# A multi-head attention block on one Trainium2 core: one output tile taken out of the planned order, and a small mask product moved from VectorE to GpSimd

## The chip, the core and the metric

The kernel runs on one core of a Trainium2 chip. A core has five engines that run side by side, each with its own instruction queue worked off in order: TensorE (PE in the profile; its weight loads are PEld), VectorE (DVE), ScalarE (ACT), GpSimd (POOL) and SyncE (SP), which here only issues DMAs. They meet through semaphores. The metric is the device time of one execution in microseconds (us); a program's time is the median over its runs.

## The reference

```python
B, S, D, H = 1, 2048, 448, 16          # x (B, S, D), wqkv (D, 3D), wo (D, D), all bf16
qkv = (x @ wqkv) -> (3, B, H, S, Dh)   # Dh = 28
scores = einsum("bhqd,bhkd->bhqk", q, k) * Dh ** -0.5
p = softmax(scores)
o = einsum("bhqk,bhkd->bhqd", p, v)
return o.reshape(B, S, D) @ wo
```

## The kernel before, in words

**Tiles.** The 16 heads form 4 groups `g` of 4 heads; the 2048 queries form 4 blocks `c` of 512 (`QW`); the keys form 16 tiles of 128. One group and one query block make a window `w = 4g + c`, 16 in all, worked off in that order. A score tile is 128 keys by 512 queries of one head (`emit_S`, L854), and there are 4 x 4 x 16 x 4 = 1024 of them. Softmax takes no maximum over scores: a bound for each key is put into spare rows of the key operand `KB` and the query operand `QB`. The key half of that bound is a mask times the largest absolute key value, `NK` (L615, 128 x 128), copied into `KB` by four DMAs (L613) for each of the groups 1 to 3.

**Exponentials.** Most score tiles come in pairs in one of two double banks `PA[0]`, `PA[1]`; ScalarE takes e^x of both at once into a tile of `PTA` (L1277, 422 times). The remaining 181 go to one of the single banks `PD[0..2]`. There VectorE and GpSimd compute the exponential together: either VectorE twice (L1058, L1061), a product on GpSimd (L1064, tile `DG`), VectorE once (L1077, tile `PTD`), 157 times; or one copy on VectorE (L990) and six GpSimd instructions (L997 to L1020), 24 times.

**Value products.** Four heads of one key tile are multiplied with the values into the accumulator bank `PO` (L1122, four matmuls side by side). At a window's end VectorE copies `PO` to `OSB` (L942), the softmax sums travel by DMA (L949, L952, L954, ending in `RRB`), and GpSimd writes the normalized result `OT[g][c]` (L957).

**Output.** For a query block `c`, four output tiles `tq` of 128 queries are each a sum over the four groups of `OT[g][c]` times `WO[:, g, :]`. `SPLIT` lists the tiles whose groups 0 to 2 are summed ahead (`task_part`, L788, kept by VectorE at L791 in unused halves of key tiles); for those `task_OP` later multiplies group 3 alone (L804) and VectorE adds the kept part (L808). For a tile that isn't in `SPLIT`, all four groups are summed in `task_OP` and VectorE copies the result (L811). One DMA on SP then writes the block's four tiles (L817).

**The end.** The last window, group 3 of block 3, has no later window to hide behind. Its groups 0 to 2 are summed into the three `PD` banks by `late_sums` (L888, output tiles 0, 1 and 3 = `ACCQ`); output tile 2 has its part in `PARTL`. Behind the last value product, code outside the planned order follows: VectorE transposes `PO` (L866), takes reciprocals (L867), and for each half of the queries transposes them back (L870) and multiplies (L1399); TensorE multiplies with `WO` (L1401), ScalarE copies tiles 0, 1, 3 (L1407), VectorE adds tile 2 (L1405), and four DMAs write them (L1408; the last from ScalarE's queue).

**Order.** Nothing is scheduled by hand or by the framework. A planner inside the kernel simulates the five engines with fixed costs for each operation (`Op`, `try_pe`, `try_act`, `try_static`, and the loop that calls them): whenever an engine is free it takes a ready operation, by `prio` and some rules of its own, so that a small change of one duration can change much of what follows. The list `log` of what was taken then becomes each engine's instruction order. At run time only that order is kept, and instructions start when their semaphores allow.

Of the kernel before, what the change touches and what calls it, by code (L numbers as in the profile page):

```python
# [10 lines left out]
ALU = mybir.AluOpType  # L11
# [7 lines left out]
P = 128  # L19
H = 16  # L20
HP = 32
G = 4
HG = 4
CC = 4
QW = 512
# [57 lines left out]
def kernel(  # L83
# [7 lines left out]
    nc = tc.nc  # L91
    _, S, D = x.shape
    Dh = D // H
    CK = D // CC
    NQC = S // QW
    NKT = S // P
    TPC = QW // P
# [53 lines left out]
    LOOK = 0.2  # L151
    SLK = 0.13
    MG = 0.1
    SPLIT = {2: (0, 1, 2, 3), 3: (2,)}
    ACCQ = (0, 1, 3)
    ACCP = 2000
    PARTD = 60
# [37 lines left out]
    out_perm = out[0][QW:S].rearrange("(p t) d -> p t d", t=NKT - TPC)  # L195
# [15 lines left out]
    WO = sb([P, G, D], BF16, "WO")  # L211
# [7 lines left out]
    KMAX = [sb([P, 1], F32, f"KMAX{g}") for g in range(G)]  # L219
    NK = [sb([P, P], BF16, f"NK{g}") for g in range(G)]  # L220
    VA = [sb([P, NKT, HG, HP], BF16, f"VA{g}") for g in range(G)]
    OT = [[sb([P, QW], BF16, f"OT{g}_{c}") for c in range(NQC)] for g in range(G)]
# [19 lines left out]
    OUTS = XS  # L242

    PA = [psum.tile([P, UA * QW], F32, name=f"PA{i}") for i in range(NA)]
    PD = [psum.tile([P, QW], F32, name=f"PD{i}") for i in range(ND)]
# [11 lines left out]
    maskm = sb([P, QW], BF16, "maskm")  # L257
# [61 lines left out]
    log = []  # L319
# [9 lines left out]
    def add(op):  # L329
        static[op.eng].append(op)  # L330
        return op

    def bank_task():
        return {"slot": None}
# [232 lines left out]
    def task_kmax(g):  # L567
        due = g * 4 * WT - 40
        prio = -4100 if g == 0 else due - 1000
        elig = None  # L570
        m = add(Op("DVE", 0.12, lambda: nc.vector.tensor_reduce(out=KMAX[g][:], in_=KPART[g][:], axis=AX.X, op=ALU.max),
                   deps=kmaxop[g], prio=prio, elig=elig))

        kmax_op.append(m)
        if g == 0:
            nk = add(Op("DVE", 0.2, lambda: nc.vector.tensor_scalar(
                out=NK[0][:], in0=maskm[:, 0:P], scalar1=KMAX[0][:, 0:1], scalar2=RK0[:, 0:1], op0=ALU.mult, op1=ALU.mult),
                deps=[m] + rk_op, prio=prio + 0.2))
            for n, (c0, c1) in enumerate(KCH):
                for i in range(HG):  # L580
                    o = add(Op("SP", DISS, (lambda i=i, c0=c0, c1=c1: nc.sync.dma_start(
                        out=KB[0][i // 2][HP * SI[i]:HP * (SI[i] + 1), c0 * QW:c1 * QW],
                        in_=KB[1][0][HP * SI[i]:HP * (SI[i] + 1), c0 * QW:c1 * QW])),
                        deps=[k0ev[sc] for sc in range(c0, c1)], prio=-2000 + 20 * n + i, lat=DLAT + 0.3))
                    k0mv.append(o)
                    for sc in range(c0, c1):
                        kev[(g, sc, i)] = o

            def rep0(i, c0, c1):
                st = SI[i] ^ 1  # L590
                nc.sync.dma_start(out=KB[0][i // 2][HP * st:HP * (st + 1), c0 * QW:c1 * QW].rearrange("p (r q) -> p r q", q=P),
                                  in_=NK[0][HP * SI[i]:HP * (SI[i] + 1), None, :].to_broadcast([HP, (c1 - c0) * QW // P, P]))
            for n, (c0, c1) in enumerate(RCH):
                for i in range(HG):
                    o = add(Op("SP", DISS + 0.07, (lambda i=i, c0=c0, c1=c1: rep0(i, c0, c1)), deps=[nk],
                               prio=(-1990 + 20 * n if c0 else -300) + 0.1 * i, lat=DLAT + 0.6, elig=None if c0 else lambda t: pos[0] >= NF * FB * HG + 4))
                    for c in range(c0, c1):
                        kmrep[(g, c, i)] = o
            return
        deps = []  # L600
        c0 = 0
        for st in (1, 3):
            o = add(Op("SP", DISS, (lambda st=st: nc.sync.dma_start(
                out=KB[g % 2][1][HP * st:HP * (st + 1), c0 * QW:S], in_=KB[g % 2][0][HP * st:HP * (st + 1), c0 * QW:S])),
                deps=[kev[(g, sc, 0)] for sc in range(c0, NQC)], prio=due + 0.01 * st, lat=DLAT + 0.3))
            deps.append(o)
            for sc in range(c0, NQC):
                kev[(g, sc, 2 + st // 2)] = o

        def rep_out(i, c0):  # L610
            st = SI[i] ^ 1
            n = (S - c0 * QW) // P
            nc.sync.dma_start(out=KB[g % 2][i // 2][HP * st:HP * (st + 1), c0 * QW:S].rearrange("p (r q) -> p r q", q=P),  # L613
                              in_=NK[g][HP * SI[i]:HP * (SI[i] + 1), None, :].to_broadcast([HP, n, P]))
        nk = add(Op("DVE", 0.2, lambda: nc.vector.tensor_scalar(  # L615
            out=NK[g][:], in0=maskm[:, 0:P], scalar1=KMAX[g][:, 0:1], scalar2=None, op0=ALU.mult), deps=[m], prio=prio + 0.2, elig=elig))
        for i in (2, 3, 0, 1):
            o = add(Op("SP", DISS + 0.07, (lambda i=i: rep_out(i, c0)), deps=[nk] + ([deps[i]] if i < 2 else []),
                       prio=due + 0.3 + 0.001 * i, lat=DLAT + 0.6))
            for c in range(c0, NQC):  # L620
                kmrep[(g, c, i)] = o
# [174 lines left out]
    def task_OP(c):  # L796
        due = (12 + c + 1) * WT + 16
        st = add(Op("SP", 0.05, None, prio=due))
        evs = []
        for tq in range(TPC):  # L800
            task = bank_task()
            ap = (lambda task=task: bank(task)[:, 0:D])
            g0 = G - 1 if c in SPLIT else 0
            ops = chain_mm(G - g0, lambda k, tq=tq, ap=ap: nc.tensor.matmul(  # L804
                out=ap(), lhsT=OT[g0 + k][c][:, tq * P:(tq + 1) * P], rhs=WO[:, g0 + k, :], start=(k == 0), stop=(g0 + k == G - 1)),
                [ot_done[(g, c)] for g in range(g0, G)], due + tq * 10, None, acq_d(task, urgent=NT - UO))
            if g0:
                ev = add(Op("DVE", 0.56, lambda tq=tq, ap=ap: nc.vector.tensor_tensor(  # L808
                    out=OUTS[c][:, tq, :], in0=ap(), in1=part(c, tq), op=ALU.add), deps=[ops[-1], parts[(c, tq)]], prio=due - 1000))
            else:  # L810
                ev = add(Op("DVE", 0.54, lambda tq=tq, ap=ap: nc.vector.tensor_copy(out=OUTS[c][:, tq, :], in_=ap()),  # L811
                            deps=[ops[-1]], prio=due - 1000))
            def aft(t, task=task):
                task["slot"].free_at = t + SEM
            ev.after = aft
            evs.append(ev)
        add(Op("SP", 0.05, lambda: nc.sync.dma_start(out=out_perm[:, c * TPC:(c + 1) * TPC, :], in_=OUTS[c][:]),  # L817
               deps=evs, prio=due))

    SEGS = [(FB * w, FB * (w + 1)) for w in range(NF)] + [(FB * NF + (NKT - FB) * w, FB * NF + (NKT - FB) * (w + 1)) for w in range(NF)]  # L820

# [18 lines left out]
    acts = []  # L840
# [22 lines left out]
    late_acc = {}  # L863

    def norm_dve(src, dt, dr, den, then):
        nc.vector.transpose(out=dt, in_=src)  # L866
        nc.vector.reciprocal(out=dr, in_=dt[:, Dh::HP])  # L867
        n = QW // HP // 2
        for hf in range(2):
            nc.vector.transpose(out=den(hf), in_=dr[:, hf * n:(hf + 1) * n].rearrange("p (n o) -> p n o", o=1).to_broadcast([P, n, HP]))  # L870
            then(hf)
# [508 lines left out]
    log.sort(key=lambda e: (e[0], e[1]))  # L1380
    sync = mybir.DependencyInfo(mybir.DependencyClass.Sync, mybir.DependencyReason.DATA)
    issued = []
    for _, _, o in log:
        if o.fn is None:
            continue
        r = o.fn()
        if o.eng == "DVE" and r is not None:
            issued.append((o, r))
        elif o.eng == "POOL" and o.kind in ("p", "n", "g"):
            before = [d for d in issued[-8:] if d[0].end <= o.start + 1e-6 and (d[0].kind == "sb" or d[0].end <= o.start - PLD + 1e-6)]  # L1390
            if before:
                tc.add_manual_dep(r.ins, before[-1][1].ins.name, sync)
    c = NQC - 1
    g = G - 1
    hw = QW // 2
    fb = {tq: PD[late_acc[tq]][:, 0:D] if tq in late_acc else PA[1 - acts[-1][2].idx][:, 0:D] for tq in range(TPC)}

    def half_out(hf):
        nc.vector.tensor_tensor(out=OTL[hf], in0=PO[:, hf * hw:(hf + 1) * hw], in1=DEN[hf], op=ALU.mult)  # L1399
        for tq in (2 * hf, 2 * hf + 1):  # L1400
            nc.tensor.matmul(out=fb[tq], lhsT=OTL[hf][:, (tq % 2) * P:(tq % 2 + 1) * P], rhs=WO[:, g, :], start=(tq not in late_acc), stop=True)  # L1401
    norm_dve(PO[:], DT[:], DR[:], lambda hf: DEN[hf], half_out)
    for tq in range(TPC):
        if tq in SPLIT[c]:
# [31 lines left out]
```

## Time and profile before

| | |
|---|---|
| time, median of 3 runs (lowest to highest) | 410.15 us (410.08 to 410.36) |
| span of the profiled execution | 408.4 us |
| ScalarE busy | 394.3 us, 97% |
| VectorE busy | 382.0 us, 94% |
| TensorE matmul busy | 359.9 us, 88% |
| GpSimd busy | 329.2 us, 81% |

The span runs from the first to the last instruction of one profiled execution; the time of a run is measured from outside and is some 1.75 us longer. An engine row gives busy time, share and instructions. In a table of groups, the part behind the bar is busy time, mean length of one, and the idle time just before such instructions with what ended it. A timeline row gives start, length, engine, line, operation, tiles, count, and in brackets the idle time before it; rows of one line that follow each other are merged, and since instructions of one engine overlap in part, the start-to-start distance can be less than the length. In the chain of waits each piece is work, or idle time marked "issue", that the end of the execution rests on.

### The profile page before, as it was taken

Reading aid. Unit: us, or ns where it says so; the run is one execution under the profiler, and the core shown is the slowest. Engines: PE = TensorE matmul, PEld = TensorE weight load, DVE = VectorE, ACT = ScalarE, POOL = GpSimd, SP = SyncE. Lnnn points to the kernel's source line nnn. Section 1 sums busy time; section 2 is a strip of 40 time slices with the busy share of each in tenths; the row PEclk is TensorE's granted clock in tenths of the full one; section 3 lists DMA queues with packets and bytes.
Section 4 is the critical chain, followed back from the end, with each engine's and each line's share of the span. In section 5 each row is a group of like instructions: output and inputs, shape, how many; then the busy total and the mean of one; then the engine's idle time right before and its main releaser. Section 6 shows DMA issues by size and latency. Waiting matters only on the chain.

```text
span 408.4 us, 7572 instructions
## 1 busy us (share of the span) xinstructions
PE 359.9 (88%) x2599; PEld 120.2 (29%) x2599; DVE 382.0 (94%) x673; ACT 394.3 (97%) x433; POOL 329.2 (81%) x352
## 2 busy tenths in 40 slices
PE   8999989798898989889898989888898988889994
PEld 5243232223233232322323232232322222223231
DVE  6996999999999999999999999999999999999985
ACT  4999999999999999999999999999999999999992
POOL 4048999778699889978697987999679988999870
PEclk9999999999999999999999999999999999999998
DMA  9251130101501020110501000010230001010112
GB/s 220 44 86 43 42 76 2 29 30 39 108 1 34 13 40 0 24 52 6 104 2 46 2 20 29 8 41 2 64 80 3 28 4 43 2 35 13 49 72 90
DMA packets 36302, 16.58 MB, mean 41 GB/s; under 512 B 28768, under 2 KB 32992, under 8 KB 36264
## 3 DMA queue, kind: packets, MB, share of 16 engines
q1 hardware_dynamic: 35656, 15.89, 16.5%
q8 instruction: 20, 0.33, 0.3%
q10 hardware_dynamic: 608, 0.22, 0.2%
q14 instruction: 18, 0.15, 0.1%
HBM read 7.44 MB, written 1.97 MB: 23 GB/s over the span
## 4 chain that ended last, share of the span: by engine, by line
ACT 55%; PE 25%; DVE 11%; issue 7%; DMA 1%; DVEq 0%; ACTq 0%
ACT PTA L1277 54%; PE PA L854 9%; PE PO L1122 7%; PE PD L854 3%; DVE DU L1058 2%; DVE DV L1061 2%; DVE PTD L1077 1%; DMA QB<-QP 1%; PE PO L652 1%; PE PA L393 1%; DVE QB L678 1%; PE PO L1238 1%; DVE QB L662 1%; DVE KB L549 1%; DVE KB L557 1%
## 5 line engine op out<-in xcount | busy, mean ns | idle before, releaser
L1277 ACT ACTIVATE PTA<-PA 128x1024 bf16<-128x1024 f32 x422 | 387.3, 1183 | 0.4 <-PE PA L854 0.2
L1064 POOL TENSOR_TENSOR DG<-DV,DU 128x512 f16<-128x512 f16 x157 | 179.9, 1156 | 49.5 <-DVE DV L1061 40.4
L854 PE MATMUL PA<-QB,KB 64*128 64x512 bf16 x843 | 168.3, 380 | 38.3 <-ACT PTA L1277 35.6
L854 PEld LDWEIGHTS <-KB 64*128 64x128 bf16 x1024 | 66.2, 93 | 180.7 <-issue 173.4
L1058 DVE TENSOR_SCALAR DU<-PD 128x512 f16<-128x512 uint16 x157 | 104.3, 680 | 7.2 <-PE PD L854 6.7
L1077 DVE SCALAR_TENSOR_TENSOR PTD<-PD,DG 128x512 uint16<-128x512 f32 x157 | 105.6, 680 | 3.1 <-POOL DG L1064 2.2
L1061 DVE SCALAR_TENSOR_TENSOR DV<-PD,DU 128x512 f16<-128x512 uint16 x157 | 104.5, 678 | 0.6
L1122 PE MATMUL PO<-PTA,VA 128*32 128x512 bf16 x843 | 86.4, 386 | 0.6 <-DVE QB L662 0.4
L854 PE MATMUL PD<-QB,KB 64*128 64x512 bf16 x181 | 65.6, 377 | 1.8 <-DVE PTD L1077 0.9
L1122 PE MATMUL PO<-PTD,VA 128*32 128x512 bf16 x181 | 52.9, 386 | 0.0
L1122 PEld LDWEIGHTS <-VA 128*32 128x32 bf16 x1024 | 19.7, 94 | 50.4 <-issue 49.7
L1003 POOL TENSOR_TENSOR GV<-GE,GU 128x512 f16<-128x512 f32 x24 | 27.8, 1159 | 2.5 <-DVE QP L691 0.8
L1005 POOL TENSOR_TENSOR GU<-GV,GU 128x512 f16<-128x512 f16 x24 | 27.8, 1156 | 1.5 <-DVE QP L691 0.8
L1007 POOL TENSOR_TENSOR SG<-SG,GU 128x512 f32<-128x512 f32 x24 | 27.8, 1157 | 1.2 <-DVE QP L691 0.6
L997 POOL TENSOR_SCALAR GU<-SG 128x512 f16<-128x512 uint16 x24 | 14.9, 619 | 7.5 <-DVE SG L990 4.7
L990 DVE COPY SG<-PD 128x512 f32<-128x512 f32 x24 | 16.4, 681 | 4.0 <-PE PD L854 3.8
L957 POOL TENSOR_TENSOR OT<-OSB,RRB 128x512 bf16<-128x512 f32 x15 | 19.1, 1273 | 0.4 <-DVE QP L691 0.4
L652 PE MATMUL PO<-XT,WQP 112*128 112x512 bf16 x56 | 18.7, 386 | 0.4 <-DVE KB L549 0.4
L1020 POOL TENSOR_SCALAR PTD<-SG 128x512 uint16<-128x512 f32 x24 | 14.9, 620 | 3.0 <-DVE QP L691 1.9
L1000 POOL TENSOR_SCALAR GE<-SG 128x512 f32<-128x512 uint16 x24 | 14.9, 619 | 1.9
L723 PEld LDWEIGHTS <-XT 112*128 112x128 bf16 x256 | 13.4, 98 | 9.4 <-issue 9.2
L522 PE MATMUL PO<-XT,WKP 112*128 112x512 bf16 x48 | 15.9, 386 | 0.0
(105 smaller groups left out, 194.2 us busy)
## 6 DMA issues: line engine op xcount, KB each, us to landing
RRB<-SCR SPq DMA_DIRECT2D x15, 256.0 KB
QB<-QP SPq DMA_DIRECT2D x56, 32.0 KB
KB<-NK SPq DMA_DIRECT2D x12, 128.0 KB
XS<-in_x_dram SPq DMA_DIRECT2D x3, 448.0 KB
out_dram<-XS SPq DMA_DIRECT2D x3, 448.0 KB
QB<-QB SPq DMA_DIRECT2D x28, 32.0 KB
KB<-KB SPq DMA_DIRECT2D x6, 128.0 KB
RRB<-SCRF SPq DMA_DIRECT2D x2, 256.0 KB
```

Source lines behind the costliest of these rows:

```text
L652: ops = chain_mm(CC, lambda cc: nc.tensor.matmul(out=ap(), lhsT=WQP[g][:, cc, :], rhs=XT[c][cc // 2][0:CK, cc % 2, :], start=(cc == 0), st ...
L854: nc.tensor.matmul(out=ap, lhsT=KB[g % 2][i // 2][a:a + 64, j * P:(j + 1) * P], rhs=QB[w % NQB][i // 2][a:a + 64, :], start=True, stop=Tru ...
L957: o5 = add(Op("POOL", 1.22, lambda: nc.gpsimd.tensor_tensor(out=OT[g][c][:], in0=OSB[b][:], in1=RRB[b][:], op=ALU.mult), deps=o4, prio=-10 ...
L1003: g3 = add(Op("POOL", PTT, lambda: nc.gpsimd.tensor_tensor(out=GV[:], in0=GE[:], in1=GU[:], op=ALU.mult), deps=[g2], prio=prio + 2, kind=" ...
L1005: g4 = add(Op("POOL", PTT, lambda: nc.gpsimd.tensor_tensor(out=GU[:], in0=GV[:], in1=GU[:], op=ALU.mult), deps=[g3], prio=prio + 3, kind=" ...
L1007: g5 = add(Op("POOL", PST, lambda: nc.gpsimd.tensor_tensor(out=X[:], in0=X[:], in1=GU[:], op=ALU.add), deps=[g4], prio=prio + 4, kind="g", ...
L1058: p1 = add(Op("DVE", P1, lambda: nc.vector.tensor_scalar(out=DU[b][:], in0=lo, scalar1=SIG / 65536, scalar2=SIG * (SS - 0.5), op0=ALU.mult ...
L1061: p2 = add(Op("DVE", P1, lambda: nc.vector.scalar_tensor_tensor(out=DV[b][:], in0=lo, scalar=65536 * (SS - 0.5 + CE / C3), in1=DU[b][:], o ...
L1064: gq = add(Op("POOL", PTT, lambda: nc.gpsimd.tensor_tensor(out=DG[b][:], in0=DV[b][:], in1=DU[b][:], op=ALU.mult), deps=[p2], prio=n, kind ...
L1077: f = add(Op("DVE", P1, lambda: nc.vector.scalar_tensor_tensor(out=PTD[st["s"].idx][:].bitcast(U16), in0=PX[slot.idx][:], scalar=EBITS + C ...
L1122: nc.tensor.matmul(out=PO[HP * st:HP * (st + 1), :], lhsT=VA[g][:, j, st, :], rhs=r["p"][i][1](), start=first, stop=last, tile_position=(0 ...
L1277: nc.scalar.activation(out=PTA[pslot.idx][:, 0:len(ns) * QW], in_=PA[s.idx][:, 0:len(ns) * QW], func=ACT.Exp, bias=ACT_BIAS, scale=ACT_SCALE)
```

## The change

Three things are edited. Output tile 3 of query block 2 leaves `SPLIT` and `task_OP`: neither its part nor its last product is planned any more. It is computed by the new `late_tile`, which is called once, right behind the last planned value product: four matmuls into the second half of the pair bank `PA` that the last ScalarE exponential doesn't use, a copy by ScalarE, and a DMA of its own on SP; the block's other three tiles go out in a smaller DMA. The three `late_sums` matmuls for output tile 3 of the last block are held back, and issued behind the first half's output products. And the mask product `NK` of groups 1 to 3 is made by GpSimd instead of VectorE. The planner's input thus changes in two places, so that the order of all engines but ScalarE differs from group 1 on.

```diff
-    SPLIT = {2: (0, 1, 2, 3), 3: (2,)}
+    SPLIT = {2: (0, 1, 2), 3: (2,)}
+    ATQ = 3
...
-        nk = add(Op("DVE", 0.2, lambda: nc.vector.tensor_scalar(
-            out=NK[g][:], in0=maskm[:, 0:P], scalar1=KMAX[g][:, 0:1], scalar2=None, op0=ALU.mult), deps=[m], prio=prio + 0.2, elig=elig))
+        nk = add(Op("POOL", 0.25, lambda: nc.gpsimd.tensor_scalar(
+            out=NK[g][:], in0=maskm[:, 0:P], scalar1=KMAX[g][:, 0:1], scalar2=0.0, op0=ALU.mult, op1=ALU.add), deps=[m], prio=prio + 0.2, elig=elig))
...
         for tq in range(TPC):
+            if c == NQC - 2 and tq == ATQ:
+                continue
             task = bank_task()
...
-        add(Op("SP", 0.05, lambda: nc.sync.dma_start(out=out_perm[:, c * TPC:(c + 1) * TPC, :], in_=OUTS[c][:]),
+        n = len(evs)
+        add(Op("SP", 0.05, lambda: nc.sync.dma_start(out=out_perm[:, c * TPC:c * TPC + n, :], in_=OUTS[c][:, 0:n, :]),
                deps=evs, prio=due))
+
+    def late_tile(ap):
+        c, tq = NQC - 2, ATQ
+        for g in range(G):
+            nc.tensor.matmul(out=ap, lhsT=OT[g][c][:, tq * P:(tq + 1) * P], rhs=WO[:, g, :], start=(g == 0), stop=(g == G - 1))
+        nc.scalar.copy(out=OUTS[c][:, tq, :], in_=ap)
+        nc.sync.dma_start(out=out_perm[:, c * TPC + tq:c * TPC + tq + 1, :], in_=OUTS[c][:, tq:tq + 1, :])
...
+    last_v = [o for _, _, o in log if o.kind == "V"][-1]
+    spare = PA[1 - acts[-1][2].idx]
+    held = []
     for _, _, o in log:
         if o.fn is None:
             continue
+        if o.kind == "A" and o.prio >= ACCP + ACCQ[-1]:
+            held.append(o)
+            continue
         r = o.fn()
+        if o is last_v:
+            late_tile(spare[:, QW:QW + D])
...
-    fb = {tq: PD[late_acc[tq]][:, 0:D] if tq in late_acc else PA[1 - acts[-1][2].idx][:, 0:D] for tq in range(TPC)}
+    fb = {tq: PD[late_acc[tq]][:, 0:D] if tq in late_acc else spare[:, 0:D] for tq in range(TPC)}

     def half_out(hf):
         nc.vector.tensor_tensor(out=OTL[hf], in0=PO[:, hf * hw:(hf + 1) * hw], in1=DEN[hf], op=ALU.mult)
         for tq in (2 * hf, 2 * hf + 1):
             nc.tensor.matmul(out=fb[tq], lhsT=OTL[hf][:, (tq % 2) * P:(tq % 2 + 1) * P], rhs=WO[:, g, :], start=(tq not in late_acc), stop=True)
+        for o in held if hf == 0 else ():
+            o.fn()
```

## The prediction, made before the changed kernel ran

> **What bounds the kernel now.** I read the table of groups first, then the waits, then the end of the execution engine by engine.
>
> ```profile
> PE 359.9 (88%) x2599; PEld 120.2 (29%) x2599; DVE 382.0 (94%) x673; ACT 394.3 (97%) x433; POOL 329.2 (81%) x352
> ...
> L1277 ACT ACTIVATE PTA<-PA 128x1024 bf16<-128x1024 f32 x422 | 387.3, 1183 | 0.4 <-PE PA L854 0.2
> ```
>
> ScalarE's 422 exponentials start every 0.92 us (387.3 / 422) from 11.3 us to 398.5 us, and ScalarE is hardly ever seen waiting among them: 0.4 us in all. In the changed kernel's instruction order ScalarE has the same exponentials in the same order. So work taken from VectorE, GpSimd or TensorE before 398.5 us buys nothing by itself; only what lies behind the last exponential, or a stall that reaches ScalarE, counts. The timeline shows the end, VectorE and ScalarE's queue first:
>
> ```profile
> 399.40 0.61 DVE L808 TENSOR_TENSOR XS<-PD,KB 128x448 bf16<-128x448 f32 x1
> 400.81 0.62 DVE L808 TENSOR_TENSOR XS<-PD,KB 128x448 bf16<-128x448 f32 x1 [0.79 <-PE PD L804]
> 401.35 0.71 DVE L866 STREAM_TRANSPOSE SG<-PO 128x512 f32<-128x512 f32 x1
> ...
> 402.86 0.42 DVE L1399 TENSOR_TENSOR QB<-PO,SG 128x256 bf16<-128x256 f32 x1
> ...
> 403.67 0.42 DVE L1399 TENSOR_TENSOR QB<-PO,SG 128x256 bf16<-128x256 f32 x1
> ...
> 405.30 0.38 ACTq L1408 DMA_DIRECT2D out_dram<-XT  x1
> ```
>
> and TensorE's rows of the same stretch:
>
> ```profile
> 399.52 0.39 PE L1122 MATMUL PO<-PTA,VA 128*32 128x512 bf16 x4
> ...
> 400.42 0.35 PE L804 MATMUL PD<-WO,OT 128*128 128x448 bf16 x1
> ...
> 404.15 0.36 PE L1401 MATMUL PA<-WO,QB 128*128 128x448 bf16 x1 [0.26 <-DVE QB L1399]
> ```
>
> The last value product (L1122) ends at 399.52 + 0.39 = 399.91. The transpose that needs it starts at 401.35, because VectorE's queue holds an L808 ahead of it, whose matmul TensorE runs only at 400.42, behind three L888. So **1.44 us of the critical end are an output tile of block 2** in VectorE's queue: 0.79 us idle, then its add.
>
> **The late tile, step by step.** In the changed order no VectorE instruction that depends on a matmul behind the last value product stands ahead of the transpose. Its start T0 is then set by the last value product. Lower bound: the last exponential ends at 399.21; a matmul group of 0.39 (L1122 row) right behind it and 0.05 for the hand-overs (L804 ends 400.77, L808 starts 400.81) give T0 = 399.7. Upper bound: in the changed order two late-sum matmuls stand ahead of the last value product, and their bank PD must first be released by the third L808, behind a PTD (L1077) that waits for the third of three GpSimd products after the last OT (L957). Now that OT starts at 394.73 with 20.5 exponential pairs left after its window; in the changed order 22.5 pairs are left, so 2 x 0.92 earlier, 392.9. Adding 1.27 (OT), 3 x 1.13 (the pair of products at 395.96 took 2.27), 0.68 (PTD), 2 x 0.58 (the two adds at 398.87 took 1.15), 0.38 (two matmuls, 0.19 apart as the six L888), 0.1 for the switch, 0.39 and 0.05 gives T0 = 400.4. I take 400.0, nearer the lower end, since the third add may well be done while TensorE still waits for the last exponential. Gain: 401.35 - 400.0 = 1.35 (bounds 0.95 to 1.65).
>
> Against it stand the added and moved instructions. TensorE, behind the last value product: four late matmuls, one and three late sums, 8 x 0.19 = 1.5 us. The first half's product becomes ready 1.93 us after T0 (403.28 - 401.35), so these are covered by 0.4 us. Then two L1401 (0.38), then the three held matmuls (0.57): the second half's first L1401 may start at 1.99 + 0.38 + 0.57 = 2.94 us after T0, and now starts 404.15 - 401.35 = 2.80 after it. **Cost 0.14.** Without the 0.4 us cover it would be up to 0.5. ScalarE: one copy of 0.53 (as L1407), from about T0 + 0.8 to T0 + 1.4; its next work, the first L1407, starts at T0 + 2.39, so it costs nothing. SP: one more DMA issue of 0.34, waiting for that copy, with the outputs of the last block queued behind it; the first of those is issued at T0 + 2.95 now (404.30), so 1.2 us of cover. If that were gone, 0.34. The last DMA goes out from ScalarE's queue and from its issue at 405.30 to the end at 408.4 takes 3.1 us as before. The sum of this part is 1.35 - 0.14 = **-1.2 us** (bounds -1.5 to -0.8).
>
> The Trainium skill, "DMA: Bandwidth & Descriptors", section "Rules for kernel authors", speaks against splitting a store: many small transfers should be merged into a large one; its section "Anatomy of one DMA" puts the fixed cost at about 2 us. The L1408 row agrees in kind (from issue at 404.30 to the last completion at 405.96, 1.7 us for 112 KB). With that cost on the path the sum would be worse by about 2 us, an estimate from the page; off the path, where the rows put it, by nothing.
>
> **The mask on GpSimd.** It leaves VectorE three times and goes to GpSimd. Rows of single lines give lengths in ns (least, median, most); the last row is from the table of groups:
>
> ```profile
> L615 DVE TENSOR_SCALAR NK<-maskm,KMAX x3: 701/704/707, 101.0 to 293.6; 128x128 bf16<-128x128 bf16 x3
> ...
> L576 DVE TENSOR_SCALAR NK<-maskm,KMAX,RK x1: 301/301/301, 20.1 to 20.1; 128x128 bf16<-128x128 bf16 x1
> ...
> L457 POOL TENSOR_SCALAR negm<-maskm x2: 197/200/203, 5.7 to 5.8; 128x16 bf16<-128x16 bf16 x2
> ...
> L1000 POOL TENSOR_SCALAR GE<-SG 128x512 f32<-128x512 uint16 x24 | 14.9, 619 | 1.9
> ```
>
> On VectorE it takes 0.70 us where a GpSimd product runs beside it, 0.30 where none does. On GpSimd, between 0.20 (16 columns) and 0.62 (512), 128 columns are about 0.30. It may have to wait for one running product, 1.16 at most, and while it waits for KMAX the products behind it in GpSimd's queue wait too, and VectorE's L1077 for them. SP's four L613 issues depend on it: at 102.35 the queue came to them 0.65 us after the mask was done, at 196.31 and 294.29 at once. So it is -0.4 to +1.1 us on those three paths; the transfers are needed by the next group's score tiles, where TensorE waited only 0.20 for one of them. I take nothing. The skill, "GPSIMD Engine Reference", section "Engine selection", gives elementwise work to VectorE, with GpSimd about half as fast on two inputs and level on one. By it the move costs up to 0.3 us each; by the 0.70 row it saves 0.4. Both are covered.
>
> **The new order of everything between.** GpSimd gets two more six-step tiles and two fewer products: 2 x (619 + 619 + 1159 + 1156 + 1157 + 620 ns) - 2 x 1156 = +8.4 us, with masks 329.2 to 338.4; VectorE loses about 6 us. Neither sets the pace. What counts are stalls that reach ScalarE. Start to start, exponentials are 0.904 apart at best; single rows show nine gaps over 0.97 after 101 us, besides five of some 1.2 that recur every 60 us whatever was ready; the nine add 1.75 us in all. Two have a named cause, both a transfer needed too soon:
>
> ```profile
> PE PD L854 <- DMA QB<-QP: 0.6, 1, 0.6
> ...
> PE PA L854 <- DMA KB<-NK: 0.2, 1, 0.2
> ```
>
> They cost ScalarE 0.46 (176.3) and 0.23 (199.4). In the changed order that query block's projection comes 23 exponential pairs ahead of its first use instead of 11, and that group's last key projection 10 ahead instead of 8. These 0.7 us should go; new stalls can come in a fresh order. I take -0.3, with all 1.75 gone as one bound and 1.0 added (six of the gaps again) as the other.
>
> **Sum.** 408.4 - 1.2 - 0.3 = 406.9 us span; with the 1.75 us between this execution and the median, **408.65 us**, 0.4% faster.
>
> **Rivals.** First, *the end gains and the body gives it back*: 1.0 us of new stalls, and 0.8 instead of 1.2 at the end, make 410.15 - 0.8 + 1.0 = 410.35; for it, GpSimd's extra 9 us and an order that no trace shows; against it, the longer leads. Second, the slower one, *the last value product gets stuck behind the late sums*: if the last OT comes no earlier than today, 394.73, the chain of the upper bound ends 1.8 us later, T0 = 402.2, the gain of 1.35 becomes a loss of 0.85, with the 0.14 1.0: 411.15. It decides from the point where the third L808 ends after 400.3 (0.92 to the transpose and the 0.14 then use up the 1.35). For it: GpSimd is fuller, and the three products follow OT directly. Against it: OT's window ends two pairs earlier. Third, *the new order also removes most stalls*: 410.15 - 1.2 - 1.4 = 407.55. Fourth, the end's wait isn't real, since TensorE is busy then anyway: excluded by the 1.13 us that L1401 waits for L1399.
>
> **Chances.** Forecast 0.55, first rival 0.16, second 0.18, third 0.10; 0.01 is left. A run tells about 0.2% (0.8 us) from no change. Faster: 0.55 + 0.10 = 0.65; same 0.16; slower 0.19. The forecast's own range is 407.9 to 409.3; the range of 8 in 10 reaches from 407.5 (third rival) to 410.6, leaving out the second.
>
> **What would show it.** Right: the transpose starts within 1.0 us of the last exponential's end, with no L808 behind the last value product; the last exponential starts between 397 and 398.8; the held matmuls sit between the two halves, and the second half's first matmul starts some 2.9 us after the transpose; NK on GpSimd takes 0.25 to 0.35. Wrong: a late-sum matmul idle before the last value product, waiting for L808; or the last exponential starting after 399.2, which would make the body, not the end, decide.

## The result: slower by 1.75%

The changed kernel takes **417.5 us** (median of 6 executions, 415.08 to 419.37), the kernel before 410.23 (6 executions, 410.08 to 410.62). The ratio is 1.0175, 95% interval 1.0151 to 1.0199. The forecast was 408.65, with a range to 410.6.

The profiled execution is the longest of the six; its span is 417.6 us, against 408.4 before. From the first exponential's start to the last one's it takes 396.93 us (11.29 to 408.22), against 387.20 (11.31 to 398.51): 9.73 us more. From there to the end it takes 9.37 instead of 9.89. So the end gained a little, and the body lost nearly twenty times that. The engine table and the groups of the changed kernel (line numbers are up to 11 higher than before: L865 is the score matmul, L1288 the exponential, L1133 the value product, L614 the mask copy):

```profile
PE 360.6 (86%) x2591; PEld 118.8 (28%) x2604; DVE 378.0 (91%) x664; ACT 395.7 (95%) x434; POOL 339.2 (81%) x365
...
L1288 ACT ACTIVATE PTA<-PA 128x1024 bf16<-128x1024 f32 x422 | 388.3, 1190 | 9.0 <-PE PA L865 8.2
```

The engines are about as busy as the prediction had them (GpSimd 339.2, forecast 338.4; VectorE 378.0, forecast some 376). What is new stands at the far right: ScalarE, which waited 0.4 us in all between exponentials, waits 9.0, and 8.2 of it for score matmuls. The table of waits says why these are late; the columns are the total, the number of times and the longest:

```profile
ACT PTA L1288 <- PE PA L865: 8.2, 7, 3.8
...
PEld L865 <- DMA KB<-NK: 6.0, 2, 3.7
PE PD L865 <- DMA KB<-NK: 5.4, 2, 3.4
```

TensorE waits twice, for `KB<-NK`, the DMA that copies the mask product into the key operand. The timeline of TensorE at the two places, the starts of groups 1 and 2:

```profile
107.79 0.39 PE L865 MATMUL PA<-QB,KB 64*128 64x512 bf16 x2
110.18 0.61 PE L865 MATMUL PD<-QB,KB 64*128 64x512 bf16 x1 [1.99 <-DMA KB<-NK]
...
205.65 0.39 PE L865 MATMUL PA<-QB,KB 64*128 64x512 bf16 x2 [0.53 <-ACT PTA L1288]
209.48 0.60 PE L865 MATMUL PD<-QB,KB 64*128 64x512 bf16 x1 [3.44 <-DMA KB<-NK]
```

The waiting matmul writes a `PD` bank: it is a tile of the next group for VectorE, which the planner takes some rows ahead of its turn. VectorE has run out of work by then and waits for it too (2.99 and 2.87 us), but that isn't what costs: TensorE works its matmuls off in order, and the pairs for ScalarE stand behind this tile. And the matmuls behind the wait take 0.61 instead of 0.39. Busy time by stretch (window and length, then PE, PEld, DVE, ACT, POOL, each with its count, then the granted clock, which is the share of its full speed that TensorE was given, DMA share, GB/s), first the changed kernel:

```profile
108.00:112.00 4.00, 2.01 (x14) 0.41 (x12) 1.18 (x2) 1.90 (x3) 1.50 (x2) 0.75 0.52 104
112.00:116.00 4.00, 4.00 (x24) 0.59 (x16) 2.87 (x6) 2.74 (x3) 3.11 (x4) 0.50 0.06 14
206.00:211.00 5.00, 1.56 (x9) 0.32 (x7) 1.94 (x4) 1.43 (x2) 0.89 (x3) 0.80 0.45 85
211.00:217.00 6.00, 6.00 (x43) 1.14 (x41) 4.10 (x7) 4.53 (x5) 5.00 (x6) 0.60 0.05 14
```

and then the kernel before, in two of these stretches:

```profile
108.00:112.00 4.00, 3.95 (x34) 1.32 (x36) 4.00 (x8) 4.00 (x5) 3.57 (x5) 1.00 0.35 77
112.00:116.00 4.00, 4.00 (x42) 1.15 (x35) 3.48 (x7) 4.00 (x6) 4.00 (x5) 1.00 0.00 1
```

From about the end of each wait on (110.18 and 209.48) the granted clock is 0.5 for 6.8 us (110.0 to 116.9 and 209.0 to 215.8 in the clock's records), and TensorE, "busy" for the whole of 112 to 116, finishes 24 matmuls instead of 42. ScalarE shows both costs at the first place:

```profile
104.89 4.69 ACT L1288 ACTIVATE PTA<-PA 128x1024 bf16<-128x1024 f32 x5
111.67 1.02 ACT L1288 ACTIVATE PTA<-PA 128x1024 bf16<-128x1024 f32 x1 [2.10 <-PE PA L865]
113.25 1.02 ACT L1288 ACTIVATE PTA<-PA 128x1024 bf16<-128x1024 f32 x1 [0.56 <-PE PA L865]
```

The wait itself delays it by 2.25 us against a spacing of 0.904; the next four exponentials come 1.2 to 1.6 us apart, which adds 2.2. At the second place it is 4.2 and 1.7. So 4.5 + 5.9 = **10.4 us** are lost at the two places, and the rest of the body is 0.6 shorter than before.

Why are the copies late? SP's queue at group 2's start, where it issues the key rows, the four mask copies and the broadcast of a softmax sum, `RRB<-SCR` (256 KB); first before, then after:

```profile
196.31 1.36 SPq L613 DMA_DIRECT2D KB<-NK  x2
197.77 0.57 SPq L954 DMA_DIRECT2D RRB<-SCR  x1
198.44 1.27 SPq L613 DMA_DIRECT2D KB<-NK  x2
```

```profile
201.74 0.65 SPq L614 DMA_DIRECT2D KB<-NK  x1
202.48 0.57 SPq L965 DMA_DIRECT2D RRB<-SCR  x1
203.15 1.97 SPq L614 DMA_DIRECT2D KB<-NK  x3
```

The broadcast has moved ahead by one copy. When a copy lands is read from its sixteen completion records (us, issue to last completion):

| | before | after |
|---|---|---|
| group 1 | 102.35 to 107.25, 103.05 to 107.71, 103.75 to 107.95, 106.52 to 109.13 | 102.20 to 106.99, 102.89 to 107.31, 106.72 to 109.26, 107.35 to 110.13 |
| group 2, ahead of the broadcast | 196.31 to 198.91, 197.06 to 199.72 | 201.74 to 204.33 |
| group 2, behind it | 198.44 to 203.94, 199.09 to 204.37 | 203.15 to 209.43, 203.81 to 209.77, 204.48 to 210.23 |

At group 2 a copy takes 2.6 us ahead of the broadcast, and 5.3 to 6.3 behind it; the last four of its sixteen completions follow 1.7 to 2.7 us after the other twelve. The tile that is taken ahead at group 2 is another one in the new order (by the kernels' instruction lists). Before, it is of head 2 and reads the copy that goes out first, ahead of the broadcast; now it is of head 1 and reads the first copy behind the broadcast, which lands at 209.43, and the matmul starts at 209.48. At group 1 the four copies go out in the order of heads 0, 2, 1, 3 instead of 0, 2, 3, 1; copy 1 has to wait for the key rows that a second `KB<-KB` moves, and copy 3, which the early tile reads (the same tile in both orders), now stands behind it: it lands at 110.13, and the matmul starts at 110.18. The planner counts on a copy 2.0 us after its issue, so in its own simulation nothing waits.

### The profile page after: what moved, and what is told of

Its sections match the earlier page's. It is cut to its first block, busy times and chain, and to the rows that moved or that the text cites. A ratio compares the mean times of both kernels' runs of the same rounds, so it can differ in the third digit from the quotient of the medians.

```text
span 417.6 us, 7577 instructions
## 1 busy us (share of the span) xinstructions
PE 360.6 (86%) x2591; PEld 118.8 (28%) x2604; DVE 378.0 (91%) x664; ACT 395.7 (95%) x434; POOL 339.2 (81%) x365
## 4 chain that ended last, share of the span: by engine, by line
ACT 52%; PE 25%; DVE 8%; issue 7%; DMA 5%; POOL 2%; SPq 1%; DVEq 0%; ACTq 0%; POOLq 0%
ACT PTA L1288 51%; PE PA L865 10%; PE PO L1133 8%; PE PD L865 3%; DMA KB<-NK 2%; DVE DU L1069 2%; DVE DV L1072 1%; DMA KB<-KB 1%; DMA WK<-in_wqkv_dram 1%; DVE PTD L1088 1%; POOL DG L1075 1%; PE PO L523 1%; DVE QB L679 1%; DVE XT L426 1%; DVE KB L550 0%
## 5 line engine op out<-in xcount | busy, mean ns | idle before, releaser
L1288 ACT ACTIVATE PTA<-PA 128x1024 bf16<-128x1024 f32 x422 | 388.3, 1190 | 9.0 <-PE PA L865 8.2
L1075 POOL TENSOR_TENSOR DG<-DV,DU 128x512 f16<-128x512 f16 x155 | 177.3, 1156 | 38.1 <-DVE DV L1072 31.8
L865 PE MATMUL PA<-QB,KB 64*128 64x512 bf16 x843 | 170.9, 384 | 42.1 <-ACT PTA L1288 39.6
L865 PEld LDWEIGHTS <-KB 64*128 64x128 bf16 x1024 | 65.7, 93 | 187.7 <-issue 173.6
L1069 DVE TENSOR_SCALAR DU<-PD 128x512 f16<-128x512 uint16 x155 | 103.1, 682 | 10.8 <-PE PD L865 10.2
L1088 DVE SCALAR_TENSOR_TENSOR PTD<-PD,DG 128x512 uint16<-128x512 f32 x155 | 104.1, 682 | 4.5 <-POOL DG L1075 4.0
L1133 PE MATMUL PO<-PTA,VA 128*32 128x512 bf16 x843 | 88.4, 396 | 0.1
L865 PE MATMUL PD<-QB,KB 64*128 64x512 bf16 x181 | 65.0, 387 | 6.3 <-DMA KB<-NK 5.4
L1133 PE MATMUL PO<-PTD,VA 128*32 128x512 bf16 x181 | 51.7, 396 | 0.3 <-issue 0.3
L1133 PEld LDWEIGHTS <-VA 128*32 128x32 bf16 x1024 | 19.4, 94 | 52.4 <-issue 52.0
L1018 POOL TENSOR_TENSOR SG<-SG,GU 128x512 f32<-128x512 f32 x26 | 30.1, 1158 | 3.3 <-DVE PTD L1088 2.5
L1014 POOL TENSOR_TENSOR GV<-GE,GU 128x512 f16<-128x512 f32 x26 | 30.1, 1157 | 2.1 <-DVE DU L1069 0.9
L1016 POOL TENSOR_TENSOR GU<-GV,GU 128x512 f16<-128x512 f16 x26 | 30.1, 1156 | 1.2 <-DVE QP L692 0.5
L1001 DVE COPY SG<-PD 128x512 f32<-128x512 f32 x26 | 17.8, 685 | 10.8 <-PE PD L865 10.5
L1031 POOL TENSOR_SCALAR PTD<-SG 128x512 uint16<-128x512 f32 x26 | 16.2, 621 | 5.1 <-DVE QP L692 3.4
```

The source lines that it names most:

```text
L865: nc.tensor.matmul(out=ap, lhsT=KB[g % 2][i // 2][a:a + 64, j * P:(j + 1) * P], rhs=QB[w % NQB][i // 2][a:a + 64, :], start=True, stop=Tru ...
L1014: g3 = add(Op("POOL", PTT, lambda: nc.gpsimd.tensor_tensor(out=GV[:], in0=GE[:], in1=GU[:], op=ALU.mult), deps=[g2], prio=prio + 2, kind=" ...
L1016: g4 = add(Op("POOL", PTT, lambda: nc.gpsimd.tensor_tensor(out=GU[:], in0=GV[:], in1=GU[:], op=ALU.mult), deps=[g3], prio=prio + 3, kind=" ...
L1018: g5 = add(Op("POOL", PST, lambda: nc.gpsimd.tensor_tensor(out=X[:], in0=X[:], in1=GU[:], op=ALU.add), deps=[g4], prio=prio + 4, kind="g", ...
L1069: p1 = add(Op("DVE", P1, lambda: nc.vector.tensor_scalar(out=DU[b][:], in0=lo, scalar1=SIG / 65536, scalar2=SIG * (SS - 0.5), op0=ALU.mult ...
L1075: gq = add(Op("POOL", PTT, lambda: nc.gpsimd.tensor_tensor(out=DG[b][:], in0=DV[b][:], in1=DU[b][:], op=ALU.mult), deps=[p2], prio=n, kind ...
```

## The experiments

Rival accounts to tell apart: the mask product itself is slow or late on GpSimd; the late tile is what hurts; the re-planned order as a whole is worse; or the account just given, that in SP's new order the copies come too late for tiles taken ahead (some expectations call it C), with a halved clock behind it. Each ratio is to the kernel before, on the same chip. Line numbers shift with the edits: the score matmul is L854, L856, L865 or L868.

**1. The late tile alone.** The changed kernel, with the mask product back on VectorE:

```diff
-        nk = add(Op("POOL", 0.25, lambda: nc.gpsimd.tensor_scalar(
+        nk = add(Op("DVE", 0.2, lambda: nc.vector.tensor_scalar(
```

> The changed kernel with the mask product back on VectorE, so only the late output tile remains. Theory C (copies): the 7 us come from the mask edit alone, whose new order makes TensorE read mask rows before their copies have landed at the starts of groups 1 and 2. Then this kernel runs in about 409.4 us (408.8 to 410.0), TensorE waits for KB<-NK under 0.5 us in all, and the transpose starts 0.6 to 0.8 us after the last exponential's end. Rival T (tail): the late tile is what slows; then 412 us or more. Rival G (GpSimd): the mask work on GpSimd itself costs; it says the same here as C.

Measured: 410.27 (12 executions), ratio 0.9987 (0.9971 to 1.0002). The late tile doesn't slow the kernel. It doesn't speed it up by what was forecast either: in this order, a third one, the last exponential is 1024 instead of 512 wide and ends 0.96 us later (400.17), and the transpose follows it by 1.26 instead of 0.72.

**2. The mask product alone.** The kernel before, with the one line of the mask edit.

> The kernel before with only the mask product moved to GpSimd. C: about 418 us (415 to 420), with two waits of TensorE for KB<-NK of 1.5 us or more near 108 and 206 us and a granted clock near 0.6 just behind each. G: the same time. T: 410.2.

Measured: 417.71, ratio 1.0152 (1.0114 to 1.0190). Its table of waits has the same two:

```profile
ACT PTA L1277 <- PE PA L854: 7.3, 7, 3.4
...
PE PD L854 <- DMA KB<-NK: 5.2, 2, 3.0
```

This one-line edit holds the whole loss.

**3. The mask product on GpSimd in the old order.** The planner is told that VectorE does it, as before; GpSimd's instruction is issued in that place.

```diff
+        def mask_on_pool():
+            nc.gpsimd.tensor_scalar(
+                out=NK[g][:], in0=maskm[:, 0:P], scalar1=KMAX[g][:, 0:1], scalar2=0.0, op0=ALU.mult, op1=ALU.add)
+        nk = add(Op("DVE", 0.2, mask_on_pool, deps=[m], prio=prio + 0.2, elig=elig))
```

> The kernel before, planned as if the mask were on VectorE, so that every engine keeps its old order, but with the three mask products issued to GpSimd. C: 410.2 us (409.8 to 410.7), no wait for KB<-NK over 0.5. G: 413 us or more, since GpSimd does the same work as in the changed kernel.

Measured: 410.46 (12 executions), ratio 0.9989 (0.9975 to 1.0003). Running it on GpSimd costs nothing; only what it does to the plan costs.

**4. A planner that knows the late landing.** The changed kernel, one number changed:

```diff
-                       prio=due + 0.3 + 0.001 * i, lat=DLAT + 0.6))
+                       prio=due + 0.3 + 0.001 * i, lat=6.3))
```

> The changed kernel, whose planner is told that a mask copy lands 6.3 us after its issue slot instead of 2.0, so that TensorE is not sent to the new keys before. C: each wait for KB<-NK under 0.5, no clock drop, 408.6 to 411 us. G: still 415 or more.

Measured: 410.4 (10 executions), ratio 0.9990 (0.9975 to 1.0006). No wait for `KB<-NK`, no clock drop. This is a new order as well, so by itself it supports the account without singling out the copies. The planner now leaves a gap of its own at group 3's start, where ScalarE waits 2.27 us for its pair; 6.3 is more than a copy takes with nothing large ahead of it (2.6), which would explain the gap, though that was not separated.

**5. The late tile in the old order.** The kernel before; the planned instructions of output tile 3 keep their place in the plan but aren't issued, and the late tile and the held matmuls follow at the end. The output is complete. The line that skips them (others collect them in `dropped`):

```diff
-        if o.fn is None:
+        if o.fn is None or id(o) in dropped:
             continue
```

> The kernel before with its planned order kept instruction by instruction; only the planned instructions of output tile 3 of block 2 are not issued, and the late tile, its copy and its DMA come behind the last value product as in the changed kernel, with the three late sums held. Theory O (order): with the tail edit alone on chip, the re-planned order gave its gain back (a last exponential of 1024 columns and more value products behind it). Then here the transpose starts 0.7 to 0.8 us after the last exponential's end, the rest of the end takes 0.15 longer, and the time is 409.0 us (408.7 to 409.4). Rival: the late tile is worth nothing itself, 410.0 or more.

Measured: median 409.56 of 11 executions, of which seven lie within 409.1 to 409.6 and four at 412.1 to 415.7; ratio 1.0000 (0.9969 to 1.0030), so no gain is shown over all of them. The four show a mean clock of 0.978 to 0.987, the others 0.998 or more; why isn't known. The profiled one, of the seven, has a span of 407.4, 1.0 less than before.

**6. Two copies swapped in the old order.** The kernel before; copies 1 and 3 of group 1 change places on SP's queue. The mask product is on VectorE, and nothing else moves.

```diff
+    copies[(1, 1)].fn, copies[(1, 3)].fn = copies[(1, 3)].fn, copies[(1, 1)].fn
```

> The kernel before with one thing changed: of the four mask copies of group 1 the third and the fourth on SP's queue change places, as they stand in the changed kernel; the mask stays on VectorE. Theory C (copies): the score tile taken ahead, which reads the copy that is now last, waits some 1.7 us near 108 us, the granted clock falls behind it, and the time is 412 to 414.5 us. Rival: the order of two copies is harmless and something else in the new order stalls; 410.5 or less.

Measured: 415.34 (4 executions, 413.60 to 417.99), above the expected window; ratio 1.0126 (1.0090 to 1.0161). But in this profile the clock was halved for 13.7 us from 104.2 on, before the wait, which was 0.66 us; the price was mixed with something else. What halved it isn't shown: TensorE has no wait over 0.53 us in the 90 us ahead. The quickest of the four, 413.60, has a mean clock of 0.996, against 0.997 in the profiled execution of the kernel before, whose clock falls only at its very end; 6.8 us at half speed would take 0.008 off the mean. So the swap seems to have cost some 3.3 us there without a drop of that length. To see the wait unmixed, the same kernel was profiled again:

> The kernel of before with only copies 1 and 3 of group 1 swapped on SP's queue, a second time. Theory: the wait for KB<-NK near 110 us is there again, and the clock drop starts behind it or just ahead of it: 413 to 418 us, clock 0.5 for 6.8 or 13.7 us. Rival (the drop had to do with something else): an execution within 1 us of before with that wait in it.

Measured: 414.96, and TensorE's timeline:

```profile
107.75 0.39 PE L856 MATMUL PA<-QB,KB 64*128 64x512 bf16 x2
110.67 0.61 PE L856 MATMUL PD<-QB,KB 64*128 64x512 bf16 x1 [2.54 <-DMA KB<-NK]
```

with a clock of 0.80 in 108 to 112, 0.50 in 112 to 116 and 0.85 in 116 to 120. The last copy lands at 110.63. Here the drop comes with the wait (it begins at 110.39), and the body is 4.87 us longer than before (392.07 against 387.20): a swap of two DMA issues, with no change to any engine's arithmetic, is worth that.

**7. The copies first.** The changed kernel; on SP's queue alone, the copies of each group go out in the order 2, 3, 0, 1, and the broadcast behind them.

```diff
+    order = [o for _, _, o in log]
+    for g_ in range(1, G):
+        four = sorted((copies[(g_, i)] for i in range(HG)), key=order.index)
+        fns = [copies[(g_, i)].fn for i in (2, 3, 0, 1)]
+        lo, hi = order.index(four[0]), order.index(four[-1])
+        for o in [o for o in order[lo:hi] if o in spreads]:
+            order.remove(o)
+            order.insert(order.index(four[-1]) + 1, o)
+        for o, fn in zip(four, fns):
+            o.fn = fn
+    log[:] = [(0, 0, o) for o in order]
```

> The changed kernel with only SP's queue rearranged at the three group starts: the two copies that the tiles taken ahead read go first (order 2, 3, 0, 1), and a broadcast of softmax sums (RRB) that stood among the four goes behind them. Mask on GpSimd, all other engines' order as in the changed kernel. C: each wait of TensorE for KB<-NK under 0.7 us, 409.5 us (408.8 to 410.8). Rival: the order of the other engines carries part of the loss, 412 or more.

Measured: 409.8 (10 executions, 409.44 to 410.45) against 410.33, ratio **0.9985 (0.9975 to 0.9995)**: a little faster than both kernels. One weight load still waits 0.7 for `KB<-NK`, at group 2, where the early tile reads copy 1, now the last of the four; no clock drop.

**8 and 9. Each place by itself.** As 7, but only group 1's copies reordered (8), or only the broadcast moved behind the copies of group 2 (9):

```diff
-    for g_ in range(1, G):
+    for g_ in (1,):
```

> The changed kernel; only group 1's four mask copies go out in the order 2, 3, 0, 1, group 2 stays as the change left it. Theory (two separate places, each a late copy with a slow clock behind it): the wait at 108-110 us and its clock drop go, the one at 206-209 us stays: 417.5 less about 4.5 = 413.0 us (412 to 414), one drop of 6.8 us in the granted clock. Rival (the second place follows from the first, as the planner's clock and the chip's have drifted apart by then): both go, about 409.8. Rival (the first place costs little): 416.5 or more.

> The changed kernel; only the RRB<-SCR broadcast at the start of group 2 goes out behind the mask copies instead of among them; the order of the copies and group 1 stay as the change left them. Theory: the copies land 2.6 us after their issue instead of 6, the wait at 206-209 us and its clock drop go, the one at 108-110 us stays: 417.5 less about 5.9 = 411.6 us (410.6 to 412.8). Rival (the copies' own order at group 2 matters, not the broadcast): about 417. Rival (what waits for RRB is hurt by the later broadcast): a new stall of 1 us or more behind 206 us, 412.6 or more.

Measured: 414.75 (414.05 to 415.21) and 413.72 (413.41 to 413.87); ratios 1.0100 (1.0082 to 1.0118) and 1.0075 (1.0059 to 1.0092). Each profile has one wait and one drop left, with a mean clock of 0.991 and 0.992. In 8 it is group 2's:

```profile
201.42 0.39 PE L868 MATMUL PA<-QB,KB 64*128 64x512 bf16 x2 [0.52 <-ACT PTA L1292]
205.03 0.60 PE L868 MATMUL PD<-QB,KB 64*128 64x512 bf16 x1 [3.22 <-DMA KB<-NK]
```

and in 9 group 1's, 1.92 us at 110.03. In 9 the four copies of group 2 land 2.6 to 2.7 us after their issue: the broadcast ahead of them was the cause there. Against 7, with neither place (387.30), the bodies are 5.2 us (392.51) and 3.9 us (391.16) longer, together 9.1, of the 9.6 that the changed kernel has. So the two places are separate. Both medians lie above the expected windows, since these were counted down from 417.5; counted up from 409.8 the places cost 5.0 and 3.9, 8.9 in all where the medians have 7.7. The changed kernel's executions differ: three have a mean clock of 0.982 or 0.983 and take 418.1 to 419.4, three have 0.987 to 0.991 and take 415.1 to 416.9. So not each of them pays for both clock drops; which pays is not shown.

**10. The late tile with TensorE's stream kept.** As 5, but the three part sums of output tile 3 are still issued, with nothing reading them.

```diff
-                dropped.update(map(id, ops + [ev]))
+                dropped.add(id(ev))
```

> The order of before with the late tile and the held matmuls at the end, as in the kernel whose four of eleven executions took 412 to 415.7 us; here the three part-sum matmuls of output tile 3 are still issued, though nothing reads them, so TensorE's stream before the end is that of before. Theory (leaving them out made TensorE idle enough at one place for the clock to be halved in some executions): no execution above 411, median 409.2 (408.9 to 409.6). Rival (the spread comes from elsewhere, the end or VectorE's shifted times): again several of the executions at 412 or more.

Measured: 409.4 (12 executions; ten at 409.2 to 409.7, one at 410.6, one at 414.42 with a clock of 0.978), ratio 0.9984 (0.9962 to 1.0006). One of twelve instead of four of eleven doesn't settle whether the part sums kept the clock up. The interval takes in 1, so a gain in time isn't shown clear of noise either; the usual time is 1.0 below before, and the end looks as forecast:

```profile
400.13 0.72 DVE L880 STREAM_TRANSPOSE SG<-PO 128x512 f32<-128x512 f32 x1
...
404.23 0.38 ACTq L1432 DMA_DIRECT2D out_dram<-XT  x1
```

## Why the prediction was wrong, point by point

**The bound was right.** ScalarE's exponentials set the pace, and "a stall that reaches ScalarE" was named as what would count. That is what came.

**The late tile: right in its mechanism, and in size up to the last DMA.** The end of the changed kernel:

```profile
409.09 0.40 PE L1133 MATMUL PO<-PTA,VA 128*32 128x512 bf16 x4
...
409.57 0.72 DVE L877 STREAM_TRANSPOSE SG<-PO 128x512 f32<-128x512 f32 x1 [1.48 <-PE PO L1133]
...
410.39 0.53 ACT L828 CAST XS<-PA 128x448 bf16<-128x448 f32 x1 [1.54 <-PE PA L827]
```

The transpose starts 0.72 us after the last exponential's end (before 2.13; forecast 0.79) and right behind the last value product, with no add ahead of it. From it to the last DMA's issue it takes 4.10 instead of 3.95: the forecast cost of 0.14 for the three held matmuls is 0.15. (The terms of the upper bound of T0 add up to 400.3, not 400.4, which changes nothing.) The copy on ScalarE and the extra DMA cost nothing, as put. (The 2 us that the prediction cites for a DMA are given on that page for those that GpSimd issues; this one is SP's, and it stayed off the path.) In experiment 10 the stretch from the last exponential's end to the end of the span goes from 9.18 to 7.87: 1.31 gained, forecast 1.2. In the changed kernel it is only 0.45, as the stretch from the last issue to the end, which the prediction kept at 3.1, takes 3.92 there.

**The mask on GpSimd: the step that failed.** Its length was nearly right (0.377 us, forecast 0.25 to 0.35), and experiment 3 shows that the move costs nothing by itself. But the step went on: the transfers "are needed by the next group's score tiles, where TensorE waited only 0.20 for one of them. I take nothing." A short wait was read as slack. It was the opposite, a race just won. TensorE in the kernel before, at the starts of groups 1 and 2:

```profile
107.83 0.39 PE L854 MATMUL PA<-QB,KB 64*128 64x512 bf16 x2
108.04 0.65 PE L854 MATMUL PD<-QB,KB 64*128 64x512 bf16 x2
...
198.91 0.39 PE L854 MATMUL PA<-QB,KB 64*128 64x512 bf16 x2 [0.20 <-DMA KB<-NK]
199.13 0.37 PE L854 MATMUL PD<-QB,KB 64*128 64x512 bf16 x1
```

Group 1's third copy lands at 107.95, and the tile taken ahead starts at 108.04; group 2's first lands at 198.91, and TensorE, which has waited for it, goes on at 198.91. With at most 0.09 us in hand, an order of SP's queue that brought the early tile's copy later had to lose. What was put at nothing measured 4.5 us at group 1 and 5.9 at group 2. The bound of +1.1 priced a mask made late. At group 1 the mask came in time (first copy issued at 102.20, before 102.35); at group 2 the new order issues it 1.2 us later even without a stall ahead (experiment 7: 197.55 against 196.31), and there it does no harm. What cost was the order of the queue behind the mask. That order stands in the changed kernel's instruction lists, and the landing times in the trace before.

**The new order: a term of -0.3 with a bound of +1.0, where the body measured +9.7.** Of the two stalls named for it, the one on `QB<-QP` did shrink (the weight load's wait from 0.9 to 0.4), and the body outside the two places became 0.6 shorter; the other, the 0.2 on `KB<-NK` at group 2, is the one that grew to 3.4. The leads were counted in exponential pairs for projections, but not for the DMA issues; and "1.0 added (six of the gaps again)" assumed that a new gap is as large as an old one. One gap was 4.2, and in the profiled execution a halved clock came with each, for which the profile before, with a granted clock of 1.00 throughout these stretches, had no row.

**The rivals.** The first, that the body gives the gain back by 1.0 of new stalls, had the right place and a tenth of the size. The slower one, the value product behind the late sums, did not happen: the transpose shows it. The sign set for "wrong", a last exponential after 399.2, came at 408.22. A loss of this size was in none of them; the chances left it 0.01.

## What to carry to other kernels

Where an order comes from a planner, an edit that costs nothing on its engine is priced by the order it leaves behind: compare each DMA queue's order before and after, and set each transfer's landing time beside the start of its first reader. A wait of 0.2 us, or none, with a landing 0.1 us ahead of the reader, is no slack but a cliff, above all on an in-order engine that has taken a tile ahead of its turn. And with a stall of TensorE of 2 us or more a slow clock behind it is to be reckoned with: in the profiled execution that added 1.7 to 2.2 us to 2.3 to 4.2.

## What the runs showed of the hardware

**The clock.** In this kernel, TensorE's seven profiled waits of 1.9 to 3.4 us for `KB<-NK` (the changed kernel, experiments 2, 8 and 9, the second profile of 6) each came with a granted clock of 0.5 for 6.8 us, which began between 2.1 us ahead of the wait's end and 1.5 us behind it; a wait of 1.0 us (experiment 3, for `QB<-QP`) had no drop with it. The wait is not the whole rule: the 13.7 us at half speed in the first profile of 6 had no such wait ahead, and the 413.60 us execution of the same kernel seems to have too high a mean clock (0.996) for a drop of 6.8 us. The Trainium skill, "TensorE: Matmul & The Clock Gate", section "What's actually happening", has a free-running window of about 3.4 us, and the stretches here are two and four of these. Its section "Why this matters for your kernels" warns of gaps over about 3 us; here drops came with waits of 1.92 us (experiment 9) and 1.99 us (group 1).

**A DMA behind a broadcast.** At group 2, a 128 KB copy issued right behind the 256 KB broadcast on the same queue completes 5.3 to 6.3 us after its issue instead of 2.6; with the broadcast moved behind the copies (experiment 9) all four take 2.6 to 2.7.

**The last completion.** In the changed kernel fifteen of the last DMA's sixteen completions are in by 415.57 and the last one at 416.47; an instruction transfer of 8,192 bytes runs on another queue from 414.83 to 415.49. The skill's "DMA: Bandwidth & Descriptors", section "Queues, rings and completion order", says that the engines serve their queues in turn and that one row of them belongs to the runtime's refills, which fits. Such a transfer near the end is seen in experiments 2, 7, 8 and 9 too, where the stretch from ScalarE's last issue to the end takes 3.74 to 4.06 us, and in none of 1, 3, 4, 5, 6 and 10, where it takes 3.0 to 3.1. That it causes the 0.6 to 1.0 us, and why it falls there, was not tried.
